# RWKV-6 attention and an MLP mixer on one core: in the fourth unit, the turned keys and the forward scan stand later in the queues

## The chip, the core and the metric

The kernel runs on one core of a Trainium2 chip. Everything is f32. The engines are TensorE (PE, with its weight load PEld), VectorE (DVE), ScalarE (ACT), GpSimd (POOL) and SyncE (SP), whose queue issues nearly all transfers. The metric is the device time of one execution in microseconds (us); less is better.

## The reference

Four sequences (B = 4) of 768 tokens, 8 heads of 48 channels. First an RWKV-6 attention, written as a recurrence over the tokens:

```python
for t in range(S):
    kt, vt, rt, wt = (k[:, :, t], v[:, :, t], r[:, :, t], w[:, :, t])
    cur = np.einsum('bhd,bhe->bhde', u[None] * kt, vt)
    y[:, :, t] = np.einsum('bhd,bhde->bhe', rt, state + cur)
    state = wt[:, :, :, None] * state + np.einsum('bhd,bhe->bhde', kt, vt)
```

Its output, put to `x` of [4, 768, 384], goes through an MLP mixer: over tokens, then over channels.

```python
xt = x.transpose(0, 2, 1)
h = np.maximum(xt @ w_tok1, 0.0) @ w_tok2     # 768 -> 256 -> 768
u = x + h.transpose(0, 2, 1)
h2 = np.maximum(u @ w_ch1, 0.0) @ w_ch2       # 384 -> 1536 -> 384
return u + h2
```

The mixer's weights come as 64-bit floats; the kernel reads their bits and makes f32 of them itself.

## The kernel before, in words

**Units of the attention.** The attention of a sequence is cut into three units of 256 tokens, so there are 12 units, numbered from 0; the fourth unit is number 3, the first of the second sequence (`UB` is 3). A unit works on chunks of 64 tokens. Its steps, each a closure that `unit(i)` returns by name:

- `ends` (DVE): a scan backwards over the decays `w` (L372, between L368 and L373) that gives each token the decay to its chunk's end; `keys` (DVE, L377) multiplies the keys by it.
- `begins` (DVE, L380): a scan forwards over the same `w`, in place; `queries` (DVE, L383) multiplies the queries by it.
- `tokens` (PE, L287): the scaled keys are turned, by eight transposes of 128x128 into two PSUM banks (`k_ps`); `copied` (ACT, L288, two pieces) takes them to `kT`.
- `carry` (PE, L303): the products of turned keys and values (`kv_ps`); `updates` (DVE, L446 and L448) make the four states of the chunks, and `scaled` (ACT, L438, four instructions for each state) multiplies a state by the decay of the next chunk. The states are a chain: `updates` and `scaled` in turn.
- `own_u` (ACT, L273), `own_gram` (PE, L257), `own_put` (DVE, L395): only in units 0 to 3, the products of each token with itself through `u`, from the keys and queries before they are scaled. `own_gram` takes two PSUM banks. After `own_put` the tile `u_rows` is loaded anew.
- `gram` (PE, L257) and `mask` (DVE, L269 in units 0 to 3) the products within a chunk; `before` (PE, L317) the queries with the states; `seen` (ACT, L329); `after` (PE, L338) the rest of the output; `taken` (ACT, L344) takes it to `x`; `ranges` (ACT, L364) two checks of the decays' range.

**The mixer of the first sequence** runs on PE at the same time. `up(s, jt)` is a channel product: three matmuls of 128x256 into one PSUM bank (`z_ps`, L545) that ACT drains with a Relu (L547). There are 24 of them for the first two thirds of the tokens, alternately `s = 0` and `s = 1`. Then come the down products (`down`, L621, two matmuls of 128x384 in each piece), whose sums DVE takes (L625). All these PSUM banks, the keys', the grams' and the outputs' (`y_ps`) are six of one pool; a tile gets a bank when the last reader of what it held is through.

**The weight conversion** goes on beside it. Conversion `to_ch[k]` takes 1 MB of bits from `spare` or `scratch` (loaded through SP, L206) in these steps: DVE masks the exponent (L209) and the mantissa (L215), ACT raises a power of two (L212), DVE adds the low half (L221), ACT takes the sign (L218) into the place of the exponent, DVE multiplies sign and power (L224) and puts the weights (L227, twice). Conversions 2 to 8 lie in the stretch of this change. The last one must be there for the ninth down piece.

**The order.** Every engine runs its queue in the order in which the steps are issued, and `strict` holds to that order. `steps(i)` lists the steps of unit `i` as pairs of a weight and a closure. `woven` merges lists: each step gets a place between 0 and 1, the sum of the weights before it and half its own over the list's whole weight, and all lists are sorted by place. So weights are not times, but a weight added at one place moves all steps of the list: those ahead of it a little earlier against the other list, those behind it later. Units 3, 4 and 5 are one list, woven with the channel products, the down products and conversions 2 to 8 of the first sequence:

```python
pieces = woven([e for i in range(UB, 2 * UB) for e in steps(i)], pieces)
```

In the text, "own gram" is `own_gram` of unit 3, "keys" its `keys`.

Of the kernel before, what the change touches and what calls it, by code (L numbers as in the profile page):

```python
# [62 lines left out]
def rwkv6_then_mixer(  # L63
# [18 lines left out]
    pe, dve, act, pool, sp = nc.tensor, nc.vector, nc.scalar, nc.gpsimd, nc.sync  # L82
# [35 lines left out]
    u_rows = const.tile([128, DM], f32, name="u_rows")  # L118
# [10 lines left out]
    def load_w(i):  # L129
        if i < NU:  # L130
            for cols in (slice(MID, WCOLS), slice(0, MID)) if i == 0 else (slice(0, WCOLS),):
                sp.dma_start(ws[i % 2][:, cols], w[i][:, cols])

    def rk_of(i):
        return rks[i if i < UB else (i - UB) % 2]

    def load_rk(i):
        if i < NU:
            for n in (1, 0):
                for rows in (slice(0, 128),) if i < 3 else (slice(0, D), slice(P, P + D)):  # L140
                    sp.dma_start(rk_of(i)[rows, ts(n, COLS)], rk[i, n, rows, :])
# [3 lines left out]
    def load_v(i):  # L145
        if i < NU:
            vs[i] = vpool.tile([128, UC, DM], f32, name="vt")
            b, j = divmod(i, UB)
            sp.dma_start(vs[i], v[b, ts(j, UC * 128), :].rearrange("(c p) e -> p c e", p=128))

    def load_near(i):
        if UB < i < NU:
            nears[i] = apool.tile([128, UC, 2, DM], f32, name="near", bufs=1)
            sp.dma_start(nears[i], near[i - UB - 1])
# [34 lines left out]
    early = [t.bitcast(u32) for t in halves]  # L189
# [515 lines left out]
    def steps(i):  # L705

        e = unit(i)
        up, by = e["updates"], e["scaled"]
        by_tokens = i > UB
        sums = e["products"] if by_tokens else [lambda: None] * 3  # L710
        some = lambda fs, c: [(c, f) for f in fs]
        return [(0.1, lambda: (i > UB and load_rk(i + 1), load_v(i + 1))), *([] if by_tokens else some(e["own_u"], 0.2)),
                (2.4, e["ends"]), (1.2, e["keys"]), (0.4, e["ranges"][0]), (2.2, e["begins"]), (1.0, e["tokens"]), (0.2, e["copied"][0]),
                *([] if by_tokens else [(1.0, e["own_gram"]), (1.3, e["own_put"]), (0.1, lambda: sp.dma_start(u_rows, u_all))]), (0.2, e["copied"][1]), (1.2, e["queries"]), (0.3, by[0]),
                (1.0, sums[0]), (1.0, e["carry"]), (1.0, sums[1]),
                (0.7, up[0]), (0.3, by[1]), (1.4, e["gram"]), (1.0, sums[2]), (0.1, lambda: load_near(i + 1)),
                (0.7, up[1]), (0.3, by[2]), (1.2, e["mask"]), (0.7, up[2]), (0.3, by[3]),
                *([(1.3, e["sums_put"])] if by_tokens else []), (0.7, up[3]),
                (0.1, lambda: load_w(i + 2)), (1.0, e["before"]), (0.1, e["seen"]), (1.5, e["ranges"][1]), (1.0, e["after"]), *some(e["taken"], 0.3)]
# [44 lines left out]
    def single(steps, n):  # L764
        return [(0.1, f) for f in (steps[5:] if n == 0 else steps[n < 3:])]
# [52 lines left out]
    for bt in range(B):  # L818
        ahead = []
        if bt == 0:  # L820
            to_ch = [single(e, n) for n, e in enumerate(to_ch)]
            both = [f for e in zip(ups[0], ups[1]) for f in e]
            ahead = woven(turned, sum(to_ch[:2], []), [(1.3, e1["ranges"][1])])
            of_weights = [(0.1, lambda n=n: weight_sums(n)) for n in range(4)]
            both = woven(both[:6], [(1.3, f) for f in e2["ranges"]]) + both[6:]
            pieces = woven(both, sum(to_ch[2:8], [])) + woven(downs[0][:6], to_ch[8]) + downs[0][6:] + downs[1][:4]
            pieces += woven(downs[1][4:] + ups[2], of_weights + [(0.1, f) for f in left_sums()]) + woven(downs[2], [(0.1, f) for f in lefts_in_place()])
            pieces = woven([e for i in range(UB, 2 * UB) for e in steps(i)], pieces)
        elif bt < B - 1:
            pieces = middle_mixing(bt)  # L830
        else:
            pieces = last_mixing()
        strict(*(f for _, f in ahead + pieces))
# [113 lines left out]
```

## Time and profile before

| | |
|---|---|
| median of 5 runs | 521.11 us (520.11 to 524.06) |
| the profiled execution | 521.77 us, span 520.1 us |
| PE busy | 491.4 us, 94% of the span |
| PE weight load busy | 428.1 us, 82% |
| DVE busy | 388.4 us, 75% |
| ACT busy | 229.7 us, 44% |
| POOL busy | 1.3 us |
| chain that ended last | PE 75%, DVE 11%, DMA 5%, ACT 5% |

The span is what the profile shows between the first and the last instruction; the execution's own time has 1.67 us around it. The mean granted clock of PE over the span is 0.985 of full speed. Busy time on PE counts pipelined matmuls. In timelines a line gives start, duration, engine, line, operation, output and inputs; in brackets stands the idle time of the engine before it and what ended that. A line of the chain of waits is start, duration and what the end hung on at that time.

### The profile page before, as it was taken

To read this page: it belongs to the slowest core of one execution; us is meant where nothing else is said; L and a number is where in the kernel's file an instruction comes from. 1 tells how busy PE (TensorE), PEld (TensorE's weight loads), DVE (VectorE), ACT (ScalarE), POOL (GpSimd) and SP (SyncE) were. 2 spreads that over 40 slices of the span, in tenths; PEclk is the share of its full clock that TensorE was granted. 3 is DMA by queue.
4 is the path that set the end of the run, shared out by engine and by line. 5 is a ranking of instruction groups with operands and counts; after the bars stand their busy time and mean duration, and the time that the engine had idled before them with its cause. 6 is when DMAs were issued, how large, how long until landed. Compare 5 with 4: busy or idle time off the path is not lost.

```text
span 520.1 us, 13317 instructions
## 1 busy us (share of the span) xinstructions
PE 491.4 (94%) x5794; PEld 428.1 (82%) x5794; DVE 388.4 (75%) x633; ACT 229.7 (44%) x533; POOL 1.3 (0%) x10
## 2 busy tenths in 40 slices
PE   3488979999999999999999999999999999999996
PEld 3466568866689868999999867999999859999996
DVE  7999798786596878987869668986858615684653
ACT  3968785671243236524335436524435414531300
POOL 0000000000000000000000000000000000000000
PEclk9789989999999999999999999999999999999999
DMA  8876548623303332121211432100000000000000
GB/s 314 313 261 191 153 145 279 178 79 115 107 35 133 92 116 79 62 70 64 63 62 62 144 94 63 61 18 15 3 32 1 18 15 1 1 2 33 0 33 33
DMA packets 20945, 46.06 MB, mean 89 GB/s; under 512 B 2128, under 2 KB 13008, under 8 KB 20880
## 3 DMA queue, kind: packets, MB, share of 16 engines
q1 hardware_dynamic: 20736, 45.14, 27.0%
q8 instruction: 47, 0.77, 0.6%
q14 instruction: 18, 0.15, 0.1%
q10 hardware_dynamic: 144, 0.00, 0.0%
HBM read 40.41 MB, written 4.72 MB: 87 GB/s over the span
## 4 chain that ended last, share of the span: by engine, by line
PE 75%; DVE 11%; DMA 5%; ACT 5%; issue 2%; SPq 1%; DVEq 0%
PE z_ps L582 18%; PE q_ps L643 12%; PE q_ps L639 12%; PE z_ps L545 8%; PE h_ps L529 5%; PE h_ps L522 5%; PE h_ps L621 4%; PE y_ps L317 2%; PE gram L257 2%; DMA w<-in_w_dram 2%; PE y_ps L338 2%; DMA rk<-in_rk_dram 2%; PE xT_ps L537 2%; DVE z L590 2%; DVE w L380 2%
## 5 line engine op out<-in xcount | busy, mean ns | idle before, releaser
L438 ACT ACTIVATE before<-state,to_end 112x48 f32<-112x48 f32 x176 | 44.5, 325 | 61.0 <-DVE state L448 57.7
L587 ACT COPY z<-z_ps 128x512 f32<-128x512 f32 x54 | 30.6, 587 | 57.4 <-PE z_ps L582 39.5
L590 DVE TENSOR_TENSOR z<-z,z_ps 128x512 f32<-128x512 f32 x54 | 35.9, 684 | 24.5 <-PE z_ps L582 15.9
L545 PE MATMUL z_ps<-xT,wch 128*128 128x256 f32 x216 | 50.5, 389 | 0.0
L599 ACT ACTIVATE z<-z 128x512 f32<-128x512 f32 x54 | 33.3, 631 | 33.1 <-DVE z L590 29.0
L545 PEld LDWEIGHTS z_ps<-xT,wch 128*128 128x128 f32 x216 | 40.7, 193 | 6.2 <-DVE wch L227 0.3
L639 PE MATMUL q_ps<-wch,z 128*128 128x192 f32 x222 | 42.9, 329 | 0.2
L643 PE MATMUL q_ps<-wch,z 128*128 128x192 f32 x222 | 43.0, 330 | 0.0
L639 PEld LDWEIGHTS q_ps<-wch,z 128*128 128x128 f32 x222 | 36.4, 190 | 0.9 <-ACT z L599 0.6
L643 PEld LDWEIGHTS q_ps<-wch,z 128*128 128x128 f32 x222 | 36.6, 190 | 0.5
L529 PE MATMUL h_ps<-h,wtok 128*128 128x384 f32 x96 | 35.1, 492 | 0.6 <-ACT h L524 0.6
L593 DVE TENSOR_TENSOR z<-z,z_ps 128x512 f32<-128x512 f32 x45 | 30.1, 685 | 6.9 <-PE z_ps L582 6.4
L522 PE MATMUL h_ps<-x,wtok 128*128 128x384 f32 x96 | 32.9, 490 | 0.0
L531 DVE TENSOR_TENSOR x<-x,h_ps 128x384 f32<-128x384 f32 x24 | 13.2, 552 | 26.1 <-PE h_ps L529 26.1
L621 PE MATMUL h_ps<-wch,z 128*128 128x384 f32 x96 | 32.4, 490 | 0.2 <-DVE wch L227 0.2
L582 PE MATMUL z_ps<-rk,wch 128*128 128x128 f32 x256 | 31.2, 275 | 0.0
L582 PEld LDWEIGHTS z_ps<-rk,wch 128*128 128x128 f32 x256 | 30.0, 192 | 0.0
L372 DVE TENSOR_TENSOR_SCAN to_end<-w,starts 112x1041 f32<-112x1041 f32 (+1 forms) x13 | 28.1, 2160 | 1.9 <-DMA w<-in_w_dram 1.5
L380 DVE TENSOR_TENSOR_SCAN w<-w,starts 112x1041 f32<-112x1041 f32 x12 | 27.9, 2322 | 0.0
L643 PE MATMUL q_ps<-scratch,z 128*128 128x192 f32 x144 | 27.9, 330 | 0.0
L621 PEld LDWEIGHTS h_ps<-wch,z 128*128 128x128 f32 x96 | 17.8, 190 | 11.6 <-DVE wch L227 0.3
L639 PE MATMUL q_ps<-scratch,z 128*128 128x192 f32 x144 | 27.3, 326 | 0.0
(181 smaller groups left out, 913.7 us busy)
## 6 DMA issues: line engine op xcount, KB each, us to landing
rk<-in_rk_dram SPq DMA_DIRECT2D x36, 192.0 KB, 3.8
near<-in_near_dram SPq DMA_DIRECT2D x8, 768.0 KB, 4.4
w<-in_w_dram SPq DMA_DIRECT2D x11, 520.5 KB, 4.8
vt<-in_v_dram SPq DMA_DIRECT2D x12, 384.0 KB, 3.4
out_dram<-o SPq DMA_DIRECT2D x24, 192.0 KB, 1.9
spare<-in_w_ch_dram SPq DMA_DIRECT2D x8, 512.0 KB, 4.5
scratch<-in_w_ch_dram SPq DMA_DIRECT2D x8, 512.0 KB, 5.2
rk<-in_rk_dram SPq DMA_DIRECT2D x6, 512.0 KB, 8.5
```

What stands on the lines that cost most here:

```text
L380: dve.tensor_tensor_scan(w_[:ROWS], w_[:ROWS], starts[:ROWS], 0.0, op0=ALU.mult, op1=ALU.add)
L438: act.mul(t[:ROWS, a], state[bt, g][:ROWS, a], by_last(c, j)[:, a:a + 1])
L522: pe.matmul(sums[i], wtok1[:, c, ts(i, 128)], x_of()[:, c, :], start=(c == 0), stop=(c == C - 1))
L529: pe.matmul(ps, wtok2[:, i, ts(c, 128)], h1[:, i, :], start=(i == 0), stop=(i == DTOK // 128 - 1))
L545: pe.matmul(ps, wch1[:, m, ts(jt, 128)], xT[:, m, ts(s, SEG)], start=(m == 0), stop=(m == DM // 128 - 1))
L582: pe.matmul(ps[:, q], lefts[r][:, ts(q, 128)], of[r], start=first and q == 0, stop=end and q == JB - 1, skip_group_check=True)
L587: act.copy(to(n), ps)
L590: dve.tensor_add(to(n), to(n), ps)
L599: act.activation(to(n), to(n), AF.Relu)
L621: pe.matmul(ps, zs[s][:, jt, ts(n, 128)], wch2[:, jt, :], start=(jt == 0), stop=(jt == NJ - 1))
L639: pe.matmul(L["q"], a[:, j, :], b[:, j, :], start=(j == 0), stop=False)
L643: pe.matmul(L["q"], a[:, j, :], b[:, j, :], start=False, stop=(j == HJ - 1))
```

## The change

Only `steps` changes, and in it only unit 3 (`by_tokens` is false for it alone among those that call `steps`). Before, its forward scan `begins` stood between `ranges[0]` and `tokens`, with a weight of 2.2. Now an empty step with a weight of 5.5 stands there, and `begins` follows `own_gram`. Units 4 and 5 keep their own order.

```diff
         some = lambda fs, c: [(c, f) for f in fs]
+        begins = (2.2, e["begins"])
+        early, late = ([begins], []) if by_tokens else ([(5.5, lambda: None)], [begins])
         return [(0.1, lambda: (i > UB and load_rk(i + 1), load_v(i + 1))), *([] if by_tokens else some(e["own_u"], 0.2)),
-                (2.4, e["ends"]), (1.2, e["keys"]), (0.4, e["ranges"][0]), (2.2, e["begins"]), (1.0, e["tokens"]), (0.2, e["copied"][0]),
-                *([] if by_tokens else [(1.0, e["own_gram"]), (1.3, e["own_put"]), (0.1, lambda: sp.dma_start(u_rows, u_all))]), (0.2, e["copied"][1]), (1.2, e["queries"]), (0.3, by[0]),
+                (2.4, e["ends"]), (1.2, e["keys"]), (0.4, e["ranges"][0]), *early, (1.0, e["tokens"]), (0.2, e["copied"][0]),
+                *([] if by_tokens else [(1.0, e["own_gram"]), *late, (1.3, e["own_put"]), (0.1, lambda: sp.dma_start(u_rows, u_all))]), (0.2, e["copied"][1]), (1.2, e["queries"]), (0.3, by[0]),
```

The list of units 3 to 5 gains 5.5 in weight, so the steps of all three units move against the mixer's pieces. Of the 24 channel products, seven instead of five stand ahead of the turned keys of unit 3, one as before between them and the own gram, then 6, 3, 5 and 2 (before 4, 3, 6, 2 and 3) between the own gram, `carry`, `gram`, `before` and `after`, and none (before 3) behind `after`. Of the down pieces, seven instead of four stand ahead of the turned keys of unit 4, and four as before between these and its `carry`. On DVE unit 3's forward scan moves from ahead of conversion 3's add (L221) to behind conversion 4's; its `own_put`, `queries` and states and the first steps of units 4 and 5 move behind more of the conversions' steps. On SP the load for conversion 6 moves ahead of the loads of `u_rows` and of unit 5's decays. From the second sequence's mixing on, the queues are as before.

## The prediction

> **What bounds the kernel now.** The page comes first: PE is busy for 94% of the span and carries 75% of the chain that ended last, DVE 11%. So the time is PE's work plus what PE stands still or runs slow. Then the list of waits of PE, longest first: after the first 60 us only one of them is long, 3.06 us before the turned keys (L287). The chain of waits in order of time shows it, and what comes behind it (start, us, what; a matmul in f32 leaves two records):
>
> ```profile
> 72.20 1.33 issue
> 73.53 1.06 PE k_ps L287 x8
> 74.60 2.46 PE z_ps L545 x6
> 77.05 1.53 PE gram L257 x64
> 78.58 5.38 PE z_ps L545 x24
> ...
> 89.12 1.09 PE gram L257 x64
> ...
> 119.08 0.69 DVE wch L227
> 119.78 0.04 issue
> 119.82 4.14 PE h_ps L621 x12
> ```
>
> The first products end at 70.47 (timeline of PE: start 63.65, 6.82 long). PE then waits until 73.53 for the keys that DVE scales at L377. Right after it one product takes 2.46 us where four take 5.38 later (1.34 each), and the own gram 1.53 where the next gram takes 1.09. The stretches by engine say why (stretch, us, PE busy, records, granted clock, DMA share, GB/s), here those of 1 us with two earlier ones of 2 us:
>
> ```profile
> 74.00:75.00 1.00, 1.00 (x8) 0.79 0.58 205
> 75.00:76.00 1.00, 1.00 (x4) 0.50 0.01 4
> 77.00:78.00 1.00, 1.00 (x38) 0.50 0.00 0
> 78.00:79.00 1.00, 1.00 (x40) 1.00 0.00 0
> ```
> ```profile
> 18.00:20.00 2.00, 1.36 (x63) 0.99 1.05 387
> 20.00:22.00 2.00, 0.00 (x0) 0.50 0.97 365
> ```
>
> The clock is halved for some 3.4 us after the gap. So the stall costs 3.06 + (2.46 - 1.34) + (1.53 - 1.09) = 4.6 us. The chain's end at 119.82 is the second thing to see: there PE waits 0.16 us for the last put of the weight conversion (L227). DVE is thus almost as late as PE in this stretch, and what PE gains before 119 is kept only if DVE's last put also comes earlier.
>
> Last the timelines of DVE and ACT (start, us, engine, line, operation):
>
> ```profile
> 72.21 1.22 DVE L377 TENSOR_TENSOR rk<-rk,to_end 112x1024 f32<-112x1024 f32 x1
> 73.35 0.69 DVE L209 TENSOR_SCALAR scratch<-spare 128x1024 uint16<-128x1024 uint16 x1
> 74.55 2.32 DVE L380 TENSOR_TENSOR_SCAN w<-w,starts 112x1041 f32<-112x1041 f32 x1
> ```
> ```profile
> 74.07 1.15 ACT L212 ACTIVATE scratch<-scratch,rebias 128x1024 uint16<-128x1024 uint16 x1 [1.88 <-DVE scratch L209]
> 75.12 1.15 ACT L364 ACTIVATE junk<-to_end,most 112x1041 uint8<-112x1041 f32 x1
> 76.27 1.11 ACT L218 ACTIVATE scratch<-spare 128x1024 bf16<-128x1024 int32 x1
> ```
>
> The keys come at 73.43, whatever PE does: DVE's queue up to L377 is the same in both kernels. ACT does nothing between 72.2 and 74.07, then three long instructions in a row.
>
> **The change, part by part.** No arithmetic is added; only the queues are reordered. I call to_ch[k] conversion k; DVE masks (L209, L215), adds (L221), waits for ACT (L212, L218), then multiplies (L224) and puts (L227 twice). The products are u1 to u24. Start-to-start prices from the rows: L209 0.60, L215 0.60 (0.72 before its own add), L221 1.11, L224 0.72, two L227 1.22, L380 2.24, L383 1.13, two L395 1.19, two L269 1.23, L446/L448 0.27, backward scan with L368 and L373 2.64; on ACT L212 1.05, L218 1.01, L364 1.15, a drain of z_ps (L547) 0.28, four L438 0.90.
>
> *Two products ahead of the keys.* u6 and u7 run from 70.47 to 73.13; the gap before the keys shrinks from 3.06 to 0.40, and the clock stays up there. u8 ends at 75.8.
>
> *A new wait at the own gram.* Its second bank is that of u6. ACT's queue has u6's drain behind the three long instructions of the last rows above (in the old order they stood before nothing that PE needed). L218 releases ACT at 77.28, the drain ends at 77.66, so the gram starts at 77.7 and PE idles 1.9 us from 75.8. It ends at 78.8. The old one ended at 78.58 with two products fewer (2 x 1.34): a lead of 2.7 - 0.2 = 2.5 us.
>
> *The scan moves behind conversion 4's add.* Before, L380 filled the time in which conversion 3 waits for ACT's signs. Now DVE stands from 75.8 to 77.4. From there: two puts until 79.4, masks and add of 4 until 81.8, L380 until 84.0, L224 and puts of 4 until 86.0, L395 until 87.2, masks of 5 until 88.4, L383 until 89.5, add 90.6, L224 and puts of 5 until 92.5, L446 92.8, masks and add of 6 until 95.2, L448 95.5. On SP the load of conversion 6 now stands ahead of u_rows and the next w; that of 7 stays behind them, and they wait for L395 and L383. All land before use (two loads take about 5 us; the seventh is free to go at 90.3 and used at 101.6). Nothing is charged for them; were the cover gone, up to 5 us of DVE's time.
>
> *A second new wait, at the products with the states (L317).* PE: u9 to u14 from 78.8 to 86.8, kv to 87.9, u15 to u17 to 92.0, gram to 93.1, u18 and u19 to 95.75. ACT drains u19 until 96.07, multiplies the second state (L438) until 96.97, makes the signs of 6 until 98.1; only then DVE goes on: L224 and puts to 100.1, the mask L269 to 101.3, the state (L448) to 101.65. The third state's four L438 end at 102.7. PE has done u20 to u22 by 99.8, and a few matmuls of L317 later it stands until 102.0: 2.0 us; L317 ends at 102.9. The old kernel was there, with three products fewer (4.0 us), at 99.35. The lead is down to 0.45.
>
> *The last put.* On ACT u22's drain, power (L212), seen (L329, 0.42), u23's drain, the check of the range (L364) and the signs of conversion 7 follow the third state from 102.6, so the signs are there at 106.9 and DVE has stood 2.8 us. L224 and puts 108.9, masks of 8 110.1, scan of the fifth unit 112.7, L377 113.85, add 114.95, L380 117.2, L224, puts: 119.2. PE has seven down products, the keys and an eighth down product done by 118.15 and waits 1.1 us. It goes on at 119.25, 0.57 before the old 119.82, but kv of the fifth unit (1.08), done by then before, is still to come. Sum: +0.5 us. After it PE had no wait in the old trace up to 145, and in the new order I find none: L625 holds DVE to 126, the states are ready by 133, PE reads them at 137; six products (8 us) now cover the sixth unit's keys, which DVE has 5.4 us after L625.
>
> So PE's idle time is 0.40 + 1.9 + 2.0 + 1.1 = 5.4 where it was 3.06 + 0.16, and 1.56 of slow clock are saved: 0.6 by this count, 0.5 by the walk.
>
> *What the clock does in the new gaps.* No row shows a gap of 1.9 to 2.0 with products on both sides. From below: a gap of 1.48 at 31.2 (timeline of PE) left the clock at 1.00. From above: the gap of 2.16 that ended at 18.59 was followed by 0.50 from 20 on, and the one of 3.06 by 0.50. A halved stretch of 3.4 us costs 1.7 (1.56 in the two rows above); the delay passes on, since ACT's signs stand behind the drains. At the second gap less of it meets PE work: 1.3. The nearest row is the 2.16, but it had another gap of 1.08 just before, so I take one loss for the two gaps, and keep none and two as bounds.
>
> The Trainium skill (TensorE: Matmul & The Clock Gate, Part 1 and "Why this matters for your kernels") says that the clock falls back only after an idle window of about 3.4 us, and to avoid gaps over some 3 us. By it neither new gap would cost anything and the sum would stay at +0.5; the halving at 20 after 2.16 us speaks against taking it as a bound.
>
> **The base.** The profiled execution took 521.77 (span 520.1 and 1.67 around it), the runs' median is 521.11, 0.66 below. No loss: 522.3 against the execution, 521.6 against the median. One loss: 524.0 and 523.3. Two: 525.3 and 524.6. I forecast the time beside the median: **523.3**.
>
> **Rivals.** *Both gaps slow the clock*, the one that ends slower: 524.6. For it: the gaps are alike (1.9 and 2.0 us) and 24 us apart. Against it: whether a gap halves the clock must hang on where it falls, as 1.48 did nothing. It decides from about 1.9 us in each.
>
> *One gap's loss does not come*, the walk stands: 521.6. For it the 1.48 row, against it the 2.16 row.
>
> *The stalls do not come*: ACT frees u6's bank and the third state earlier than I work out, so PE keeps 2.66 of the gap, 1.56 of slow clock and the 0.16 at 119.8, 4.4 in all: 516.7. DVE would allow it, if it never waited for ACT: 119.2 less the 7 us of idle above (1.6, 2.6, 2.8) is 112.2, and PE arrives at 119.7 - 4.2 - 1.1 = 114.4. For it: ACT is busy only 44%. Against it: ACT's order is fixed, and L212 cannot start before L209 at 73.35. It decides if u6's drain ends before 75.8. With only the second wait gone: 2.0 less, 519.6.
>
> *The change does nothing*: excluded, since the keys do stand behind 21 matmuls of the products instead of 15.
>
> **Numbers.** One loss 0.36, none 0.16, both 0.25, no stalls 0.18, second wait alone gone 0.05. About 0.5% (2.6 us) is what a measurement of this kernel can tell from no change: below 518.5 and above 523.7. Of the likeliest case, whose own range is 522.3 to 524.3, a third lies above 523.7, and a tenth of the none case. Faster 0.18, same 0.43, slower 0.39. The range runs from 517.0 (no stalls, with 0.3 of the slow clock lost elsewhere) to 526.0 (both losses and 1.4 of error in the walk).
>
> **What the new profile would show.** Right: the keys at 73.5 after a gap under 0.5; a gap of about 1.9 before the own gram, released by ACT's z L547 or L218; L317 waiting about 2 us for L438; a wait of 1 us for wch L227 near 118; granted clock 0.50 after one of the gaps. Wrong: no gap at the gram, or L317 without one, and the last L227 before 117; then it is faster. If all gaps are there and the clock stays at 1.00, the clock step was wrong.

## The result

| | before | changed |
|---|---|---|
| median of the runs | 522.84 us (94 runs) | 524.52 us (52 runs) |
| least | 520.11 us | 522.79 us |
| ratio | | 1.004 (95% interval 1.0027 to 1.0054) |
| the profiled execution | 521.77 us, span 520.1 | 524.47 us, span 522.8 |

The changed kernel is slower by 0.4%. The ratios here and below are taken over undisturbed runs alone, the medians over all, so that a ratio need not be that of two medians. The 523.3 of the forecast stood beside a median of 521.11 over five runs, which is a ratio of 1.0042; with the runs that came later the median before rose to 522.84.

The page of the changed kernel looks the same: PE 493.1 us busy (94%), DVE 388.0, ACT 229.8, the same number of matmuls. The chain that ended last has PE at 73% and DVE at 16%, where DVE had 11%.

The chain of waits in order of time, changed kernel (start, us, what):

```profile
73.42 0.61 DVE scratch L209
...
76.35 1.00 ACT scratch L218
77.35 0.28 ACT z L547
77.62 0.04 issue
77.67 1.15 PE gram L257 x62
78.82 9.65 PE z_ps L545 x36
...
103.13 0.25 DVE state L448
...
103.40 0.34 ACT before L438
...
103.79 0.99 PE y_ps L317 x28
...
119.87 1.30 DVE wch L227 x2
121.17 0.04 issue
121.22 4.14 PE h_ps L621 x12
```

Where the old chain had one long stop, this one has three: the own gram behind ACT's drain, the matmuls with the states behind the third state, and the ninth down piece behind the last put. PE's timeline gives their lengths (in brackets the idle time and what ended it):

```profile
73.52 1.06 PE L287 MATMUL k_ps<-ident,rk 128*128 128x128 f32 x8 [0.47 <-issue]
74.42 1.46 PE L545 MATMUL z_ps<-xT,wch 128*128 128x256 f32 x6
75.81 0.33 PE L257 MATMUL gram<-rk,near 48*64 48x64 f32 x2
77.67 1.15 PE L257 MATMUL gram<-rk,near 48*64 48x64 f32 x62 [1.53 <-ACT z L547]
78.75 9.72 PE L545 MATMUL z_ps<-xT,wch 128*128 128x256 f32 x36
...
101.33 0.67 PE L317 MATMUL y_ps<-before,rk 48*64 48x48 f32 x20
103.79 0.99 PE L317 MATMUL y_ps<-before,rk 48*64 48x48 f32 x28 [1.79 <-ACT before L438]
...
121.22 4.14 PE L621 MATMUL h_ps<-wch,z 128*128 128x384 f32 x12 [1.18 <-DVE wch L227]
```

The wait ahead of the turned keys is gone but for 0.47, and 0.47 + 1.53 + 1.79 + 1.18 = 4.97 us of waiting stand where there were 3.06 + 0.16. Two records of the own gram, one matmul, ran at once; the second matmul waited for the second bank. A group that is interrupted also takes longer itself: the own gram 0.33 + 1.15 us where an uninterrupted gram takes 1.16 (the line of 75.86 under e6), the matmuls with the states 0.67 + 0.99 where this line of the kernel before has 1.24:

```profile
98.11 1.24 PE L317 MATMUL y_ps<-before,rk 48*64 48x48 f32 x48
```

That is 0.32 + 0.42 = 0.74 us which no list of waits shows. Six products behind the own gram took 9.72 us, where at 1.34 they would take 8.0. The stretches of 1 us (fifth column: granted clock) say why:

```profile
79.00:80.00 1.00, 1.00 (x4) 0.70 0.78 256
80.00:81.00 1.00, 1.00 (x4) 0.50 1.12 389
81.00:82.00 1.00, 1.00 (x4) 0.50 1.10 375
82.00:83.00 1.00, 1.00 (x4) 0.59 0.92 322
```

The halved stretch of 3.4 us is there again, one wait later. After the 1.79 us at 102 the clock stayed at 1.00.

DVE's and ACT's timelines at the same place:

```profile
72.20 1.22 DVE L377 TENSOR_TENSOR rk<-rk,to_end 112x1024 f32<-112x1024 f32 x1
73.33 0.69 DVE L209 TENSOR_SCALAR scratch<-spare 128x1024 uint16<-128x1024 uint16 x1
...
77.38 0.69 DVE L224 TENSOR_TENSOR scratch<-scratch 128x1024 bf16<-128x1024 bf16 x1 [1.50 <-ACT scratch L218]
```
```profile
74.06 1.15 ACT L212 ACTIVATE scratch<-scratch,rebias 128x1024 uint16<-128x1024 uint16 x1 [1.87 <-DVE scratch L209]
75.11 1.15 ACT L364 ACTIVATE junk<-to_end,most 112x1041 uint8<-112x1041 f32 x1
...
76.25 1.09 ACT L218 ACTIVATE scratch<-spare 128x1024 bf16<-128x1024 int32 x1
77.25 0.91 ACT L547 ACTIVATE z<-z_ps 128x256 f32<-128x256 f32 x3
```

The keys come when they came before. ACT's queue runs as before too, only that the drain at its end is now the one that PE needs.

### The profile page after: what moved, and what is told of

It reads as the page before. It is cut to its first block, busy times and chain, and to the rows that moved or that the text cites. A ratio compares the mean times of both kernels' runs of the same rounds, so it can differ in the third digit from the quotient of the medians.

```text
span 522.8 us, 13319 instructions
## 1 busy us (share of the span) xinstructions
PE 493.1 (94%) x5794; PEld 429.4 (82%) x5794; DVE 388.0 (74%) x633; ACT 229.8 (44%) x533; POOL 1.3 (0%) x10
## 4 chain that ended last, share of the span: by engine, by line
PE 73%; DVE 16%; ACT 5%; issue 3%; DMA 2%; SPq 0%; DVEq 0%
PE z_ps L582 18%; PE q_ps L643 12%; PE q_ps L639 12%; PE z_ps L545 7%; PE h_ps L529 5%; PE h_ps L522 4%; PE h_ps L621 4%; PE y_ps L317 2%; PE gram L257 2%; DVE w L380 2%; DVE to_end L372 2%; PE kv_ps L303 2%; PE y_ps L338 2%; PE xT_ps L537 2%; DVE z L590 2%
## 5 line engine op out<-in xcount | busy, mean ns | idle before, releaser
L545 PE MATMUL z_ps<-xT,wch 128*128 128x256 f32 x216 | 50.5, 391 | 0.0
L545 PEld LDWEIGHTS z_ps<-xT,wch 128*128 128x128 f32 x216 | 41.5, 195 | 6.5 <-DVE wch L227 0.3
```

Of the source, the lines that this page charges most:

```text
L545: pe.matmul(ps, wch1[:, m, ts(jt, 128)], xT[:, m, ts(s, SEG)], start=(m == 0), stop=(m == DM // 128 - 1))
```

## The experiments

The start of an execution varies by more than a microsecond (the first product begins between 63.6 and 65.2 us), and a halved stretch comes or not. So beside the ratios I compare the profiled executions by the span less the start of the first product, "the rest", with what the granted clock did from 64 to 122 us:

| kernel | rest, us | halved stretch, us |
|---|---|---|
| before | 520.1 - 63.65 = 456.45 | 3.4, after the 3.06 wait |
| changed | 522.8 - 63.64 = 459.16 | 3.4, after the 1.53 wait |
| changed, again (e10) | 524.3 - 65.18 = 459.12 | 3.4, after the 1.53 wait |
| e1, scan ahead of the keys' transposes | 526.4 - 63.66 = 462.74 | 7, after a 3.75 wait |
| e2, scan alone moved | 520.9 - 64.40 = 456.50 | 3.4, after a 3.05 wait |
| e3, check moved | 522.4 - 64.65 = 457.75 | 3.4, after a 1.79 wait |
| e4, states first | 520.9 - 64.55 = 456.35 | none |
| e5, changed, waits filled | 522.2 - 64.78 = 457.42 | none |
| e6, before, wait filled | 518.5 - 63.69 = 454.81 | none |
| e7, e3 and e4 | 519.9 - 64.63 = 455.27 | none |
| e8, three edits | 518.5 - 64.29 = 454.21 | none |
| e9, three edits again | 517.8 - 63.62 = 454.18 | none |

The two pairs of equal kernels agree within 0.04 us.

**e1: the seven products, but the scan in its old place in the list.** On DVE it then stands right behind the keys, ahead of conversion 3's masks (L209, L215); in the kernel before it stood behind them.

```diff
-        early, late = ([begins], []) if by_tokens else ([(5.5, lambda: None)], [begins])
+        early, late = ([begins], []) if by_tokens else ([begins, (3.3, lambda: None)], [(2.2, lambda: None)])
```

> The changed kernel with the forward scan (L380) put back ahead of the turned keys; the empty weight is 3.3 there and 2.2 at the scan's new place, so all other steps stand as in the changed kernel. On DVE the scan then stands right behind the keys (L377), ahead of conversion 3's mask (L209). Theory (the own gram waits for ACT's drain of the sixth product, which follows conversion 3's power, which follows that mask): the mask, the drain and the own gram come 2.24 us later, the gap ahead of the own gram grows from 1.5 to some 3.7 us, and the kernel takes about 2 us more than the changed one: 1.008 times the kernel before, 1.004 without the changed kernel's loss added twice. First rival (the amount of work on DVE up to the last put sets the end): the same work in another order, so no difference from the changed kernel, 1.004. Second rival (the moved scan is what made the changed kernel slower): 1.000 or less.

Measured: 1.0113 times before (1.0063 to 1.0163). PE's timeline has the line that the theory asked for:

```profile
79.92 1.98 PE L257 MATMUL gram<-rk,near 48*64 48x64 f32 x62 [3.75 <-ACT z L547]
```

The own gram waits 3.75 instead of 1.53 us: 2.22 more, the 2.24 by which the scan holds back conversion 3's mask, and with it ACT's power, sign and drain. The cost was more than expected, 3.58 us in the rest, because the clock was halved for 7 us instead of 3.4 (the rest of the own gram took 1.98 us where it took 1.15). That it is slower, not equal, speaks against DVE's amount of work as the bound, and putting the scan back to this place made the kernel worse, not better. A place behind conversion 3's masks, where the old queue had it, was not tried with the seven products.

**e2: the scan alone.**

```diff
-        early, late = ([begins], []) if by_tokens else ([(5.5, lambda: None)], [begins])
+        early, late = ([begins], []) if by_tokens else ([(2.2, lambda: None)], [(0.01, e["begins"])])
```

> The kernel before with the forward scan alone moved behind the own gram; an empty step keeps its weight in the old place, so the turned keys stay behind five products. Theory (the two more products and what they shift make the difference, the scan fits where DVE waits anyway): the queries come 1.8 us later, conversion 4's puts 0.7 us later, and conversion 5 then waits for ACT as before: 1.000 times the kernel before, within 0.001. Rival (the scan fills a wait of DVE in its old place, and its 2.24 us come on top in the new one): up to 2.2 us more, 1.004.

Measured: 0.9992 (0.9965 to 1.0019), and the rest differs from before by 0.05 us. On DVE conversion 4's multiply comes 0.8 us later against the first product, conversion 5's not at all: it waits for ACT. The scan's move costs nothing by itself here, and gains nothing (it stands behind conversion 3's puts, in the changed kernel behind conversion 4's add). The difference lies with the two products ahead of the keys and what the empty weight of 5.5 moves.

**e3: a check out of the drain's way.**

```diff
-            both = woven(both[:6], [(1.3, f) for f in e2["ranges"]]) + both[6:]
+            both = woven(both[:6], [(1.3, e2["ranges"][0]), (1.3, lambda: None)]) + both[6:15] + [(0.01, e2["ranges"][1])] + both[15:]
```

> The changed kernel with one ACT instruction moved: the third unit's second range check (L364, 1.15 us) goes from between conversion 3's power and sign to behind the drain of a product twelve us later. Theory: the sixth product's drain ends 1.15 us earlier, the own gram's wait falls from 1.5 to about 0.4 us, its clock is not halved afterwards, and the lead passes through the chain of drains, signs and states: 1.15 us less, with the halved clock 2.8 us: 0.998 to 0.995 times the changed kernel, 1.002 to 0.999 times the kernel before. Rival (DVE's work up to the last put sets the end): 1.004, as the changed kernel. Rival (the same instruction delays as much where it goes): 1.004 too, but with the wait ahead of the own gram gone.

Measured: 1.0029 (0.9998 to 1.0061). The three longest waits of PE between 62 and 160 us:

```profile
PE y_ps L317 <- ACT before L438: 1.8, 1, 1.8
PE h_ps L621 <- DVE wch L227: 1.2, 1, 1.2
PE gram L257 <- ACT z L547: 0.6, 1, 0.6
```

The wait ahead of the own gram fell to 0.60 and the clock stayed up behind it. But in this execution it was halved behind the second wait, from 102.1 to 105.6: two products (L545) took 3.99 us where they took 2.86. The rest is 1.41 below the changed kernel's, each with one halved stretch. The time alone does not decide it (the interval reaches from no change of the kernel before to the changed kernel); the wait and the rest do.

**e4: the third state ahead of the mask.**

```diff
-                (0.7, up[1]), (0.3, by[2]), (1.2, e["mask"]), (0.7, up[2]), (0.3, by[3]),
+                *([(0.7, up[1]), (0.3, by[2]), (1.2, e["mask"]), (0.7, up[2]), (0.3, by[3])] if by_tokens else
+                  [(0.7, up[1]), (0.3, by[2]), (0.7, up[2]), (0.3, by[3]), (1.2, e["mask"])]),
```

> The changed kernel with the fourth unit's mask (L269, two of them, 1.23 us) put behind its third state's sum (L448) instead of ahead of it. Theory (the matmuls with the states wait for the third state): L448 and the third state's four L438 come 1.23 us earlier, the wait in L317 falls from 1.8 to 0.6 us, and what follows up to the last put comes 1.2 us earlier: 1.2 us less than the changed kernel, 1.002 times the kernel before. Rival (the end is set by DVE's work, not by this wait): the same as the changed kernel, 1.004, with a longer wait for the last put. Rival (the mask, now later, holds the matmuls L338 instead): 1.004.

Measured: 1.0015 (0.9982 to 1.0049). Again the three longest waits:

```profile
PE gram L257 <- ACT z L547: 1.5, 1, 1.5
PE h_ps L621 <- DVE wch L227: 1.2, 1, 1.2
PE y_ps L317 <- ACT before L438: 0.6, 1, 0.6
```

The second wait fell from 1.79 to 0.60 and the third kept its length, so the gain was not given back there. Against e5, the changed kernel without a halved stretch, the rest is 457.42 - 456.35 = 1.07 us less. Here the same wait of 1.53 us ahead of the own gram was not followed by a halved stretch; the last section shows what differed.

**e5 and e6: PE kept busy in the waits.** A few matmuls whose results nobody reads, in the changed kernel's two waits and in the old kernel's one.

```diff
+    def fill(n):
+        t = ps_a.tile([128, 2, 512], f32, name="kv_ps", tag="a")
+        for _ in range(n):
+            pe.matmul(t[:, 0, :256], ident, wtok1[:, 0, :], start=True, stop=True)
```

In e5 it stands ahead of the own gram, and six more stand in `across`, ahead of the matmuls with the states (`extra` is 6 for the fourth unit, 0 for the others):

```diff
+            plain_gram = e["own_gram"]
+            e["own_gram"] = lambda: (fill(3), plain_gram())
...
+        for _ in range(extra):
+            pe.matmul(y[0][:, X * D:], ident, wtok1[:, 0, :128], start=True, stop=True, skip_group_check=True)
```

In e6 it stands ahead of the turned keys:

```diff
+            plain = e["tokens"]
+            e["tokens"] = lambda: (fill(6), plain())
```

> The changed kernel with idle matmuls in its two new waits of PE: three of 128x256 (some 1.3 us) into the unused bank of kv ahead of the own gram, and six of 128x128 (some 1.3 us) into unused columns of the output's bank ahead of the matmuls with the states. No step of the kernel waits for them and their results are read by nobody. Theory of the clock (a wait of 1.5 to 1.9 us on PE halves the granted clock for 3.4 us in some executions): the granted clock stays at 1.00 from 64 to 118 us, the own gram, the third state and the last put come when they came, less what the halved clock cost in the changed kernel's profile (1.6 us): the most frequent time falls from 524.5 to some 522.9, 1.001 to 1.002 times the kernel before. Rival (the clock does not hang on these waits): halved stretches stay and the time is that of the changed kernel, 1.004. Rival (the idle matmuls delay what follows): slower than 1.004.

> The kernel before with six idle matmuls of 128x256 (some 2.7 us) in its 3.06 us wait ahead of the turned keys, their results read by nobody. Theory of the clock: the wait stays but PE is busy in it, no halved stretch from 74 to 78 us; one product (2.46) and the own gram (1.53) fall back to 1.34 and 1.09. PE is then 1.6 us earlier; DVE's last put, which in the kernel before came just in time, moves with the drains that ACT's signs stand behind: 0.5 to 1.6 us less, 0.999 to 0.997 times the kernel before. Rival (DVE's last put does not move): PE waits for it, 1.000, with a wait of about 1.6 us for L227. Rival (the clock does not hang on the wait): 1.000, clock halved as before.

Measured: e5 1.0044 (1.0008 to 1.008), e6 0.9993 (0.9964 to 1.0023). The times decide nothing: each interval holds the theory's ratio (1.001 to 1.002 and 0.997 to 0.999) and its rival's (1.004 and 1.000), and e5's value lies with the rival. The least times are 522.75 us in e5 and 522.79 in the changed kernel, 520.20 in e6 and 520.11 before: the best executions of the unfilled kernels were as fast as the filled ones, which fits a halving that some executions do not have. These least times stand 522.79 - 520.11 = 2.68 us apart. The profiles show more, one of each kernel. The stretch from 64 to 122 us in e6 and then in e5:

```profile
64.00:122.00 58.00, 57.38 (x584) 1.00 0.52 165
```
```profile
64.00:122.00 58.00, 55.31 (x522) 1.00 0.51 156
```

In the kernel before and in the changed kernel this stretch had 0.97. In e6 the keys' transposes, the product and the own gram follow each other at full speed:

```profile
70.35 2.75 PE L708 MATMUL kv_ps<-wtok,ident 128*128 128x256 f32 x12
73.56 1.06 PE L287 MATMUL k_ps<-ident,rk 128*128 128x128 f32 x8 [0.46 <-issue]
74.47 1.46 PE L545 MATMUL z_ps<-xT,wch 128*128 128x256 f32 x6
75.86 1.16 PE L257 MATMUL gram<-rk,near 48*64 48x64 f32 x64
```

The rest is 456.45 - 454.81 = 1.64 us shorter in e6 and 459.16 - 457.42 = 1.74 in e5: that is the price of one halved stretch, by one profile in each of two kernels. DVE's last put moved along in e6 (the ninth down piece at 118.28, 0.16 of wait as before). And without any halved stretch the changed kernel stands 457.42 - 454.81 = 2.61 us behind the old one.

**e7, e8 and e9: the waits taken away.** e7 has the edits of e3 and e4. e8 moves one more instruction, the fourth unit's second range check, which stood ahead of conversion 7's sign on ACT:

```diff
-                (0.1, lambda: load_w(i + 2)), (1.0, e["before"]), (0.1, e["seen"]), (1.5, e["ranges"][1]), (1.0, e["after"]), *some(e["taken"], 0.3)]
+                (0.1, lambda: load_w(i + 2)), (1.0, e["before"]), (0.1, e["seen"]), (1.5, e["ranges"][1] if by_tokens else lambda: None), (1.0, e["after"]), *some(e["taken"], 0.3), *([] if by_tokens else [(0.01, e["ranges"][1])])]
```

> The changed kernel with both edits: the third unit's second range check out from between conversion 3's power and sign, and the fourth unit's mask behind its third state's sum. Theory (the two new waits each pass their length on): the own gram waits 0.6 instead of 1.5 us, L317 0.6 instead of 1.8 us, no halved clock in this stretch; 0.9 + 1.2 us less than the changed kernel without a halved clock (some 522.9): about 520.7 us, 0.997 to 0.998 times the kernel before. Rival (DVE's work up to the last put sets the end): the wait for L227 grows by what the other two lose, 1.003.

> The kernel with both edits and a third: the fourth unit's second range check (L364, 1.15 us on ACT) goes from ahead of conversion 7's sign to behind the output's copies. Theory (DVE's last put is late because it waits for ACT's signs): conversion 7's multiply comes 1.15 us earlier, the last put too, and PE's wait for it falls from 1.2 to about 0: 1.1 us less than with the two edits, some 519.6 us, 0.995 times the kernel before. Rival (something else on ACT or DVE takes the place): the same as with the two edits.

> The kernel with the three edits once more, beside the changed kernel on one chip. Theory: the three new waits were the changed kernel's loss and without them its two products ahead of the keys pay: some 519.6 to 520.5 us, 0.995 to 0.998 times the kernel before. Rival (the first look was chance): 1.000.

> The changed kernel itself, for the direct comparison with the one with three edits. Theory: 1.004 times the kernel before, some 3.2 us more than with the three edits (0.9 and 1.2 and 1.1 of waits; more where a wait halves the clock). Rival: less than 1.5 us between the two.

Measured: e7 0.9982 (0.9954 to 1.0009), e8 0.9965 (0.9935 to 0.9996), the same kernel again as e9 0.9981 (0.9952 to 1.001), and the changed kernel beside it 1.0054 (1.0029 to 1.0079). In the rest e7 is 2.15 us below e5; by e3's wait (1.53 to 0.60) and e4's rest the two edits alone were worth 0.93 and 1.07, 2.00 together. e8 is 1.06 below e7. All of PE's waits between 62 and 160 us in e8:

```profile
PE y_ps L317 <- ACT before L438: 0.6, 1, 0.6
PE gram L257 <- ACT z L547: 0.6, 1, 0.6
PE k_ps L287 <- issue: 0.5, 1, 0.5
PE xT_ps L537 <- DVE x L531: 0.3, 1, 0.3
```

The wait for the last put is gone. The version with three edits is faster than the changed kernel (rest 454.2 against 459.1; medians 519.85 and 525.56 us on the same chip, and the intervals of e9 and e10 do not meet). Without the one halved stretch of the changed kernel the rest differs by 457.42 - 454.2 = 3.2 us, as e10's expectation had it. Against the kernel before it is 2.2 us less in the rest where that one has a halved stretch, and 0.6 less than e6, where the stretch is filled away; in the times e8 lies just below 1 (0.9996 at the upper end), e9's interval holds 1, so they leave a gain over the kernel before open.

## Why the prediction was right

Each of its waits was there with the releaser that it named, and their sizes came within 0.4 us. That 1.004 meets 1.0042 so closely is partly luck: in the profiles the span grew by 2.7 us where 2.2 was forecast.

- *The gap ahead of the keys*: 0.40 was expected, 0.47 measured.
- *The own gram behind the drain of u6*: a drain at 77.66 was expected and came at 77.63. The wait was 1.53 instead of 1.9, because the gram's first matmul, whose bank was free, ran from 75.81 to 76.14; the forecast counted from the end of u8 at 75.8, which was right.
- *The matmuls with the states*: 2.0 expected, 1.79 measured. e4 shows the mechanism: with the mask's 1.23 us behind the third state, 1.19 less wait.
- *The last put*: 1.1 expected, 1.18 measured; e8 takes it away at its cause, ACT's sign of conversion 7.
- *The sum without the clock in the new kernel*: +0.5 against the execution of before. By e5 it is 457.42 - 456.45 = +0.97. The walk was short by 0.47 us in all. About 0.3 of it lies ahead of the last put: in e5 the ninth down piece begins 120.71 - 64.78 = 55.93 us after the first product, forecast was 119.25 - 63.65 = 55.60. About 0.2 is in PE's way from the last put to the second third of the products: 147.24 - 121.22 = 26.02 us after and 144.57 - 119.82 = 24.75 before, 1.27 where kv alone was counted with 1.08. The forecast's second count, by idle time (+0.6), agreed with the walk by luck: with the measured 4.97 us of waiting it gives 4.97 - 3.22 - 1.56 = +0.19, since it leaves out that interrupted groups take 0.74 longer.
- *The clock*: one halved stretch for the two gaps, at 1.7 us, was the weakest step, taken between two bounds. Measured were 1.74 and 1.64 us for one stretch, and one stretch in each of the two profiles of the changed kernel. So +0.5 + 1.7 = 2.2 against +2.7 in span. That it was one, and not none or two, was not worked out; by the last section it hangs on where the waits fall. How often the timed executions had it is not known.

The rival in which the stalls do not come fell with the first profile. Its condition, the drain of u6 before 75.8, failed since ACT's queue has its order; that ACT is busy 44% of the span said nothing about it. The rival of two losses did not come in a profile; a halved stretch after the second wait does occur (e3), so executions with both are possible, but none was seen.

The rule of the Trainium skill that was weighed (TensorE: Matmul & The Clock Gate, "Why this matters for your kernels": no gaps over some 3 us) would have left the clock alone here. Waits of 1.53 us (changed kernel, twice) and 1.79 us (e3) were followed by a clock of 0.50, so measurement decides against it as a bound.

What stays open: how often each kernel has the halved stretch when no profile is taken, and so how much of the measured 0.4% is the clock's.

## What to carry to other kernels

A bubble on the bounding engine is filled by moving work ahead of it only if the buffers of that work come free in time: look up, in the queue of the engine that drains them, what stands ahead of the drain. A reordered list moves every later step too, so follow the next few handovers (here a state chain and a weight conversion that was just in time) until the lead is spent or safe. When two engines run that close, moving a long instruction which nobody waits for out of a queue that somebody waits for, as the range checks here, can be worth nearly its whole length: a check of 1.15 us gave 0.93 us of wait in e3 and 1.06 us of the rest in e8.

## What the hardware showed beyond that

Waits of 1.53 us (changed kernel, twice) and 1.79 us (e3) on PE were followed by a granted clock of 0.50 for 3.4 us, 1.6 to 1.7 us of time; a wait of 3.75 us by one for 7. The same 1.53 in e4, and the 1.79 in both profiles of the changed kernel and in e1, were not. The traces show what sets them apart. In all twelve profiles, up to 122 us, the granted clock changes only at times that lie a whole number of 3.41 us apart, a grid that starts elsewhere in each execution (in the changed kernel at 17.96, 28.20, 79.40 and 82.82: 3, 15 and 1 times 3.41). What counted between 62 and 122 us was how much of a wait fell into one stretch of this grid:

| profile | clock changes at, us | wait of PE, us | of it in one stretch of the grid, us | clock in the next stretch |
|---|---|---|---|---|
| changed | 17.96, 28.20, 79.40, 82.82 | 76.14 to 77.67 | 1.52 | 0.50 |
| changed, again (e10) | 18.90, 29.14, 32.56, 39.38, 80.34, 83.76 | 77.69 to 79.22 | 1.52 | 0.50 |
| e4 | 16.78, 30.43, 40.67, 44.09 | 77.07 to 78.60 | 1.15, then 0.37 | 1.00 |
| e3 | 20.22, 30.46, 33.87, 37.28, 102.14, 105.55 | 100.38 to 102.17 | 1.75 | 0.50 |
| changed | as above | 102.00 to 103.79 | 1.30, then 0.49 | 1.00 |

In the twelve profiles every stretch at full clock there with 1.52 us or more of idle PE was followed by a halved one (six), and none with 1.30 or less. By these numbers a wait of 1.53 us lies whole in one stretch at (3.41 - 1.53) / 3.41 = 55% of the places that it can have, an estimate. Idle time is not the whole rule: before 62 us, where PE's matmuls are small, e4 has a halving behind 1.11 us of idle time and e2 none behind 1.56. Why e1's lasted two stretches is not shown.

Matmuls without a purpose in the wait kept the clock at 1.00 in the one profile of each filled kernel (e5, e6). They held nothing up: in e6 the turned keys begin 73.56 - 63.69 = 9.87 us after the first product, before 73.53 - 63.65 = 9.88. In the timed runs no gain is shown (1.0044 in e5, 0.9993 in e6).
